# Splitting converted weights on GpSimd, and one attention product moved ahead, in a chunked-attention and gated-MLP kernel

## The chip, the cores and the metric

The kernel runs on one core of a Trainium2 chip. The core has five engines that work side by side, each with its own queue in order: TensorE (PE, matrix products), VectorE (DVE), ScalarE (ACT), GpSimd (POOL) and SyncE (SP, which here only issues DMAs). They work on SBUF, an on-chip memory of 128 partitions, and on PSUM, the banks into which PE writes. The metric is the time of one execution in microseconds (us) of device time.

## The reference

There are two parts. The first is attention within chunks of 64 positions, for 8 batches and 8 heads of 576 positions and 64 dimensions:

```
scores = scale * np.matmul(q_c, k_c.transpose(0, 1, 2, 4, 3))
attn = np.exp(scores - max); attn = attn / (sum + 1e-9)
out = np.matmul(attn, v_c)
```

Its result is read as x, 4608 tokens of 512 features. The second part is a gated MLP with 1536 hidden features:

```
gate = 1.0 / (1.0 + np.exp(-(x @ w_gate)))
val = x @ w_val
return (gate * val @ w_out).astype(np.float32)
```

All is float32. The weights are handed to the kernel as float64 bit patterns, two 32-bit words for each number.

## The kernel before

**Precision.** PE multiplies a 32-bit format with a shorter mantissa (float32r). So each factor of an MLP product is held as two parts, hi and lo: hi is the number cast to float32r, lo is what the cast left out. Each product is then three: hi with hi, hi with lo, lo with hi.

**Conversion of weights.** The weights are cut into 12 tiles f of 128 hidden features, and each tile has three parts of 128 x 512 numbers: gate (part 0), value (1) and out (2). `load_weights` (L99) brings a part's two words a number into a raw buffer by SP (L108). `convert_weights` (L110) makes hi and lo of it, in seven instructions: two multiplications by powers of two on ACT (L129, L130), a shift (L131), an and/or (L132) and an add (L134) on DVE, which together give the float32 number `val`; then the cast to hi on ACT (L136) and the subtraction val - hi = lo on DVE (L137). There are 36 conversions. For tiles 0 to 8 `val` lies in buffers of the weight pool that later tiles will use; from tile 9 on it lies in the pool `mp` under the tag "ob", which has two buffers. The raw buffers alternate too, so that the load of one tile's words waits for the conversion of an earlier one.

**Attention.** The work is cut into 36 units j = (block m of 512 tokens, half h of the block, group u of 4 heads). For a unit, `scores` (L177) multiplies q and k on PE (`products`, L170), takes the maximum on DVE, and either subtracts it there (op "S") or does subtraction, exponential and sum on ACT (op "s"); `softmax` ("E", L198) finishes the probabilities; `transposes` ("T" or "t", L211) turns them on PE and copies them back; `values` ("A", L224) multiplies by v (L231), and casts and subtracts the result into the hi and lo parts of x (L249 on ACT, L250 on DVE). Scores, transposes and products of values share two PSUM buffers (`ps_a`) in turn.

**MLP.** `hidden` ("H", L267) makes one tile f of hidden features for a block, or for one half ("a", "b") of it: 12 products with the gate weights (L261), a sigmoid on ACT (L270), 12 products with the value weights, the product of the two on DVE (hf, L272), and its hi (L274, ACT) and lo (hl, L276, DVE). `down` ("D", L281) multiplies these by the out weights into four accumulators (L287). Hidden features of tile f need all parts 0 and 1 of that tile, the down products need part 2.

**Order.** The strings START and MIDDLE list the first block's operations by hand: L and V are loads of q, k and v, W loads of weights ("u" for parts 0 and 1, "o" for part 2), C conversions ("C3.1" is part 1 of tile 3). In START, a planner that knows a cost for each instruction may still reorder each engine's queue, with the order of the string as priority. In MIDDLE the order of PE is as written and the other engines are planned; after it (`rest`, L642) PE and DVE are both as written.

**After the first block.** Blocks 1 and 2 go tile by tile in the same manner. Meanwhile POOL makes sums of the hi and lo weights (`keep_sums`, L331: L338, L344, a cast L346 and a subtraction L347), SP writes the weights and sums to DRAM (L324, L329), and blocks 3 to 8 are then done two at a time by a scheme with seven products in place of eight (L421, L496).

Of the kernel before, what the change touches and what calls it, by code (L numbers as in the profile page):

```python
# [8 lines left out]
F32 = mybir.dt.float32  # L9
# [3 lines left out]
ALU = mybir.AluOpType  # L13
# [13 lines left out]


START = """
L0 L1 V0 W0o S0 s1 V1 E0 W0u t0 C0.0 E1 L2 t1 L3 C0.1 A0 W1u S2 C0.2 s3 A1 C1.0 H0.0a E2 W1o E3 C1.1  # L30
T2 W2u T3 D V3 L4 V2 C2.0 A2 C1.2 A3 L5 H0.1a H0.0b W3o D W3u C2.1 C3.0 H0.1b D s4 W4u W2o H0.2 C3.2
C2.2 W4o C3.1 C4.0 D W5u E4 C4.1 C5.0 C5.1 H0.3 D s5 C4.2 t4 E5 W6u H0.4 D W7u C6.0 V5 W6o C7.0 C6.1
H0.5 D W5o L6 C5.2 L7 C6.2 H0.6 V4 W8u C7.1 D W7o C8.0 t5 C8.1 C7.2 H0.7 D W9u
# [15 lines left out]
def chunk_attn_moe(ctx: ExitStack, tc: tile.TileContext, q, k, v, w, out):  # L49


    nc = tc.nc
# [43 lines left out]
    def stage(tag, n):  # L96
        return wp.tile([P, n], U32, tag=tag, name="w_raw")
# [12 lines left out]
    def convert_weights(f, part):  # L110

        words = raws.pop((f, part)).rearrange("p (n two) -> p two n", two=2)
        low, high = words[:, 0, :], words[:, 1, :]
        if part == 0:
            both = wp.tile([P, 2, 1024], F32R, tag=f"u{f}", name="w")
            wt[f, 0], wt[f, 1] = both[:, :, :512], both[:, :, 512:]
        elif part == 2:
            wt[f, 2] = wp.tile([P, 2, 512], F32R, tag=f"o{f}", name="w")
        hi, lo = wt[f, part][:, 0], wt[f, part][:, 1]
        if f < 9:  # L120
            slot = 9 if f == 8 else 9 - f % 2
            if part == 0:
                spare[f] = stage(f"u{slot}", 2048)
            val = stage(f"o{slot}", 1024)[:, :512] if part == 2 else spare[f][:, 512 * part:512 * (part + 1)]
        else:
            val = mp.tile([P, 512], U32, tag="ob", name="w_val")


        nc.scalar.mul(val.bitcast(F32), high.bitcast(F32), 2.0 ** -112)  # L129
        nc.scalar.mul(low, low, 2.0 ** -29)  # L130
        nc.vector.tensor_scalar(out=val, in0=val, scalar1=3, scalar2=None, op0=ALU.logical_shift_left)  # L131
        nc.vector.scalar_tensor_tensor(  # L132
            out=val, in0=high, scalar=0x80000000, in1=val, op0=ALU.bitwise_and, op1=ALU.bitwise_or)
        nc.vector.tensor_tensor(out=val, in0=val, in1=low, op=ALU.add)  # L134
        val = val.bitcast(F32)
        nc.scalar.copy(hi, val)  # L136
        nc.vector.tensor_tensor(out=lo, in0=val, in1=hi.bitcast(F32), op=ALU.subtract)  # L137


    units = [(m, h, u) for m in range(NB) for h in range(2) for u in range(2)]  # L140
# [464 lines left out]
    def run(op):  # L605
        what, arg = op[0], op[1:]
        if what == "L":
            load(int(arg))
        elif what == "V":
            load_values(int(arg))  # L610
        elif what in "Ss":
            scores(int(arg), what == "s")
        elif what == "E":
            softmax(int(arg))
        elif what in "Tt":
            transposes(int(arg), what == "t")
        elif what == "A":
            values(int(arg))
        elif what == "W":
            load_weights(int(arg[:-1]), arg[-1])  # L620
        elif what == "C":
            f, part = arg.split(".")
            convert_weights(int(f), int(part))
        elif what == "H":
            m, f = arg.split(".")
            step(int(m), int(f.rstrip("ab")), f.lstrip("0123456789"))
        else:
            finish()
# [115 lines left out]
```

## Time and profile before

| what | value |
|---|---|
| median of 3 runs | 948.76 us (946.94 to 950.25) |
| the profiled execution | 949.0 us, of which span 947.2 us |
| PE busy | 927.4 us (98%) |
| DVE busy | 601.1 us (63%) |
| ACT busy | 340.5 us (36%) |
| POOL busy | 139.0 us (15%) |
| granted PE clock, mean | 0.994 |

The span runs from the first instruction to the last; the profiled execution's own time has 1.8 us around it. In the rows of the profile, "L137" is a line of the kernel, "lo<-val,hi" would name the tile written and those read, and "x18" a count of instructions. In the time line an instruction's start and duration stand first, and the idle time of its engine ahead of it, with what ended it, in square brackets. Buffer names: `w` is a weight's hi and lo pair, `w_raw` the raw words (and, for tiles 0 to 8, `val`), `w_val` is `val` of tiles 9 to 11.

### The profile page before, as it was taken

How to read it: one execution, taken by the hardware profiler on the slowest of the kernel's cores; microseconds unless marked ns; L12 is line 12 of the kernel's file. 1: busy time of each engine (PE TensorE's matmuls, PEld its weight loads, DVE VectorE, ACT ScalarE, POOL GpSimd, SP SyncE). 2: the span in 40 equal slices, each digit the busy share in tenths (PEclk: the TensorE clock that was granted, in tenths of full speed). 3: DMA queues.
4: the chain of work that ended last, by engine and by line, in shares of the span. 5: the costliest groups of instructions: out<-in, count | busy, mean ns of one | idle time of the engine just before them, and what ended most of it. 6: DMA issues, size and time to landing. Idle time of an engine off the chain costs nothing.

```text
span 947.2 us, 13080 instructions
## 1 busy us (share of the span) xinstructions
PE 927.4 (98%) x4960; PEld 762.0 (80%) x4960; DVE 601.1 (63%) x999; ACT 340.5 (36%) x556; POOL 139.0 (15%) x204
## 2 busy tenths in 40 slices
PE   6999999999999999999999999999999999999998
PEld 4778888888888887888887888888878888888886
DVE  6899973576576656766766666767686334445332
ACT  6899752233233242233142522232324221121222
POOL 1000006970079880000000000000000000000000
PEclk7999999999999999999999999999999999999999
DMA  8699894442243448657675756665565565556561
GB/s 290 210 305 298 313 305 168 134 145 78 64 137 112 134 141 312 203 200 229 205 246 207 254 186 219 211 220 201 190 222 197 193 208 183 203 184 215 218 222 45
DMA packets 81279, 189.61 MB, mean 200 GB/s; under 512 B 7488, under 2 KB 38208, under 8 KB 76608
## 3 DMA queue, kind: packets, MB, share of 16 engines
q1 hardware_dynamic: 81216, 188.77, 59.5%
q8 instruction: 39, 0.64, 0.3%
q14 instruction: 24, 0.20, 0.1%
HBM read 150.99 MB, written 37.75 MB: 199 GB/s over the span
## 4 chain that ended last, share of the span: by engine, by line
PE 81%; POOL 6%; DMA 6%; ACT 3%; DVE 2%; issue 1%; SPq 1%; POOLq 0%; ACTq 0%; DVEq 0%
PE acc L496 20%; PE cy L421 16%; PE g L261 13%; PE cz L421 11%; PE cx L421 10%; PE acc L287 6%; DMA sums<-a_both 3%; PE sc L170 3%; PE av L231 3%; POOL a_both L347 2%; POOL a_sum L344 2%; POOL a_both L346 1%; POOL a_val L338 1%; DMA out<-ob 1%; DMA wr<-sums 1%
## 5 line engine op out<-in xcount | busy, mean ns | idle before, releaser
L261 PE MATMUL g<-xt,w 128*128 128x512 f32 (+1 forms) x960 | 207.5, 371 | 3.0 <-ACT xt L249 1.3
L261 PEld LDWEIGHTS g<-xt,w 128*128 128x128 f32 x960 | 168.5, 189 | 36.3 <-ACT xt L249 1.7
L496 PE MATMUL acc<-wr,hh 128*128 128x512 f32 x576 | 177.8, 390 | 0.0
L421 PE MATMUL cy<-xc,wr 128*128 128x512 f32 x648 | 159.2, 389 | 0.9 <-DVE u L439 0.9
L421 PEld LDWEIGHTS cy<-xc,wr 128*128 128x128 f32 x648 | 121.5, 188 | 26.5 <-DVE u L439 1.3
L496 PEld LDWEIGHTS acc<-wr,hh 128*128 128x128 f32 x576 | 107.9, 188 | 22.7 <-ACT raw L242 0.3
L496 PE MATMUL acc<-wr,hl 128*128 128x512 f32 x288 | 112.7, 391 | 2.7 <-DVE hl L488 2.7
L421 PE MATMUL cz<-xc,wr 128*128 128x512 f32 x432 | 106.1, 391 | 1.1 <-DMA wr<-sums 1.1
L421 PE MATMUL cx<-xc,wr 128*128 128x512 f32 x432 | 106.0, 391 | 0.0
L560 DVE STREAM_TRANSPOSE pbd<-pr 32x256 f32<-32x256 f32 x224 | 97.6, 436 | 4.0
L488 DVE TENSOR_TENSOR hl<-hid,hh 128x512 fp32r<-128x512 f32 x72 | 49.5, 688 | 78.8 <-ACT hh L486 78.5
L421 PEld LDWEIGHTS cz<-xc,wr 128*128 128x128 f32 x432 | 80.5, 188 | 19.0 <-issue 2.5
L421 PEld LDWEIGHTS cx<-xc,wr 128*128 128x128 f32 x432 | 80.6, 188 | 17.5 <-issue 1.0
L287 PE MATMUL acc<-w,hh 128*128 128x512 f32 x288 | 90.4, 395 | 1.0 <-ACT hh L274 1.0
L486 ACT CAST hh<-hid 128x512 fp32r<-128x512 f32 x72 | 44.8, 622 | 127.1 <-PE acc L496 103.7
L338 POOL TENSOR_TENSOR a_val<-w 128x256 f32<-128x256 f32 x48 | 37.3, 798 | 202.2 <-ACT xt L249 144.7
L496 PEld LDWEIGHTS acc<-wr,hl 128*128 128x128 f32 x288 | 54.0, 188 | 16.0 <-DVE hl L488 4.8
L439 DVE TENSOR_TENSOR u<-cy,s 128x512 f32<-128x512 f32 x36 | 24.8, 688 | 63.3 <-PE cy L421 61.3
L272 DVE TENSOR_TENSOR hf<-g,hf 128x512 f32<-128x512 f32 (+1 forms) x40 | 25.4, 635 | 60.6 <-PE g L261 59.6
L287 PEld LDWEIGHTS acc<-w,hh 128*128 128x128 f32 x288 | 52.7, 188 | 13.1 <-issue 1.9
L456 DVE TENSOR_TENSOR u<-cy,s 128x512 f32<-128x512 f32 x36 | 24.9, 691 | 50.7 <-PE cy L421 50.5
L287 PE MATMUL acc<-w,hl 128*128 128x512 f32 x144 | 56.1, 389 | 0.0
(103 smaller groups left out, 1009.4 us busy)
## 6 DMA issues: line engine op xcount, KB each, us to landing
wr<-sums SPq DMA_DIRECT2D x72, 512.0 KB, 4.6
wr<-outer SPq DMA_DIRECT2D x36, 1024.0 KB, 4.9
w_raw<-w_in SPq DMA_DIRECT2D x36, 512.0 KB, 5.0
wr<-given SPq DMA_DIRECT2D x36, 512.0 KB, 3.7
sums<-a_both SPq DMA_DIRECT2D x24, 512.0 KB, 3.5
qt<-q_in SPq DMA_DIRECT2D x36, 256.0 KB, 4.4
kbd<-k_in SPq DMA_DIRECT2D x72, 128.0 KB, 4.4
vt<-v_in SPq DMA_DIRECT2D x36, 256.0 KB, 4.0
```

What stands on the lines that cost most here:

```text
L170: nc.tensor.matmul(sc[c * D:(c + 1) * D, (2 * a + t) * P:(2 * a + t + 1) * P], lhsT=s["qt"][:, a, n0:n0 + D], rhs=s["kb"][:, a, :, n0:n0 + D],
L231: nc.tensor.matmul(av[a * D:(a + 1) * D, c * P:(c + 1) * P], lhsT=s["vt"][:, a, c, :], rhs=pb[:, 4 * a + c, :, :], start=True, stop=True,)
L261: nc.tensor.matmul(ps[:, tok], lhsT=wt[f, which][:, wpart, c:c + P], rhs=x[:, part, i, tok], start=n == 0, stop=n == 11)
L272: nc.vector.tensor_tensor(out=hf, in0=pv, in1=hf, op=ALU.mult)
L287: nc.tensor.matmul(acc[m, t], lhsT=hx[:, ts], rhs=wt[f, 2][:, wpart], start=f == 0 and i == 0, stop=f == NF - 1 and i == 2,)
L338: nc.gpsimd.tensor_tensor(out=val[:, 2 * n:2 * n + 2], in0=parts[:, 0], in1=parts[:, 1], op=ALU.add)
L421: nc.tensor.matmul(bank, lhsT=lhs(wpart, c), rhs=x[:, part, c], start=start and k == 0, stop=stop and k == 5, skip_group_check=True)
L456: nc.vector.tensor_tensor(out=u3, in0=y, in1=s1, op=ALU.add)
L486: nc.scalar.copy(hh, h)
L488: nc.vector.tensor_tensor(out=hl, in0=h, in1=hh.bitcast(F32), op=ALU.subtract)
L496: nc.tensor.matmul(acc[m, t], lhsT=hx[:, ts], rhs=wo[f][:, wpart], start=f == 0 and i == 0, stop=f == NF - 1 and i == 2)
L560: nc.vector.transpose(out=pb[dst, :, c, h, i, :], in_=ps[src, h::2, k, :])
```

## The change

Two things are changed. First, in `convert_weights`, the cast to hi and the subtraction for lo go from ACT and DVE to POOL, for all conversions but the first (tile 0, part 0). Second, in the string START, the operation A1 (the product of unit 1's probabilities with v) stands right behind A0, ahead of W1u, S2, C0.2 and s3, where before it stood behind them.

```diff
-L0 L1 V0 W0o S0 s1 V1 E0 W0u t0 C0.0 E1 L2 t1 L3 C0.1 A0 W1u S2 C0.2 s3 A1 C1.0 H0.0a E2 W1o E3 C1.1
+L0 L1 V0 W0o S0 s1 V1 E0 W0u t0 C0.0 E1 L2 t1 L3 C0.1 A0 A1 W1u S2 C0.2 s3 C1.0 H0.0a E2 W1o E3 C1.1
...
         val = val.bitcast(F32)
-        nc.scalar.copy(hi, val)
-        nc.vector.tensor_tensor(out=lo, in0=val, in1=hi.bitcast(F32), op=ALU.subtract)
+        if (f, part) == (0, 0):
+            nc.scalar.copy(hi, val)
+            nc.vector.tensor_tensor(out=lo, in0=val, in1=hi.bitcast(F32), op=ALU.subtract)
+        else:
+            nc.gpsimd.tensor_copy(hi, val)
+            nc.gpsimd.tensor_tensor(out=lo, in0=val, in1=hi.bitcast(F32), op=ALU.subtract)
```

## The prediction

> **What bounds the kernel now.** The time slices of the page show TensorE (PE) full from the third slice of 23.7 us on: time can only be won or lost where it would stop. So I asked next for the table by stage, over the stretch where the weights are converted. Its columns are start and end, length, busy time of PE, weight loads, VectorE (DVE), ScalarE (ACT) and GpSimd (POOL), granted clock, DMA share and GB/s:
>
> ```profile
> 8.00:56.00 48.00, 39.78 (x300) 33.21 (x296) 41.36 (x86) 40.14 (x106) 0.00 (x0) 0.89 0.80 262
> 56.00:124.80 68.80, 68.80 (x330) 56.42 (x330) 64.84 (x119) 57.67 (x112) 0.00 (x0) 1.00 0.92 311
> ```
>
> From 8 to 56 us PE idles 48.00 - 39.78 = 8.2 us and is led by DVE and ACT, both over 80% busy. From 56 us on PE never stops, yet DVE is 64.84 / 68.8 = 94% busy, and POOL does nothing. Whether DVE has anything in hand shows where the last up tile (f = 11) takes its weights, in the timelines of DVE and PE:
>
> ```profile
> 123.41 1.46 DVE L137 TENSOR_TENSOR w<-w_val,w 128x512 fp32r<-128x512 f32 x2
> 124.81 5.60 PE L261 MATMUL g<-xt,w 128*128 128x512 f32 x24
> ```
>
> The gate and value weights of tile 11 are finished at about 124.1 and at 124.87. PE takes the gate half at 124.81 and the value half 2.8 us later: 0.7 and 2.7 us in hand. The conversions thus run at PE's pace, and whatever slows them by more than that stops PE.
>
> **The move to GpSimd.** Thirty-five of 36 conversions give their cast (L136) and subtraction (L137) to POOL. The groups of 56 to 124.8 us, counts behind "x", mean ns behind the comma:
>
> ```profile
> L137 DVE TENSOR_TENSOR w<-w_raw,w 128x512 fp32r<-128x512 f32 x18 | 12.2, 686 | 1.7 <-ACT w L136 1.7
> L134 DVE CUSTOM_DVE_ANT_0 w_raw<-w_raw 128x1024 uint16<-128x1024 uint16 x15 | 10.2, 683 | 0.0
> L132 DVE SCALAR_TENSOR_TENSOR w_raw<-w_raw 128x512 uint32<-128x512 uint32 x15 | 10.1, 685 | 0.0
> L131 DVE TENSOR_SCALAR w_raw<-w_raw 128x512 uint32<-128x512 uint32 x15 | 6.0, 420 | 0.0
> L132 DVE SCALAR_TENSOR_TENSOR w_val<-w_raw,w_val 128x512 uint32<-128x512 uint32 x8 | 5.5, 688 | 0.1
> L137 DVE TENSOR_TENSOR w<-w_val,w 128x512 fp32r<-128x512 f32 x8 | 5.5, 687 | 0.3 <-ACT w L136 0.2
> L134 DVE CUSTOM_DVE_ANT_0 w_val<-w_raw,w_val 128x1024 uint16<-128x1024 uint16 x8 | 5.5, 686 | 0.1
> L276 DVE TENSOR_TENSOR hl<-hf,hh 128x512 fp32r<-128x512 f32 x8 | 5.4, 680 | 0.1
> L131 DVE TENSOR_SCALAR w_val<-w_val 128x512 uint32<-128x512 uint32 x8 | 3.3, 424 | 1.4 <-ACT w_val L129 1.3
> ```
>
> Here 18 + 8 = 26 subtractions leave DVE, 12.2 + 5.5 = 17.7 us; the casts leave ACT. POOL's price for the same shapes and types is in its own later work (minimum/median/maximum ns):
>
> ```profile
> L346 POOL CAST a_both<-a_sum x24: 606/611/1614, 152.8 to 349.4; 128x512 fp32r<-128x512 f32 x24
> L347 POOL TENSOR_TENSOR a_both<-a_sum,a_both x24: 1275/1291/2150, 154.1 to 350.9; 128x512 fp32r<-128x512 f32 x24
> ```
>
> Alone, POOL needs 0.61 + 1.29 = 1.90 us a conversion, 26 x 1.90 = 49.4 us of the 68.8: it would fit. The maxima say what goes wrong. Rows of POOL and DVE that overlap:
>
> ```profile
> 269.61 0.73 POOL L338 TENSOR_TENSOR a_val<-w 128x256 f32<-128x256 f32 x1
> 270.30 1.29 POOL L347 TENSOR_TENSOR a_both<-a_sum,a_both 128x512 fp32r<-128x512 f32 x1
> 271.55 1.19 POOL L338 TENSOR_TENSOR a_val<-w 128x256 f32<-128x256 f32 x1
> ...
> 277.31 1.30 POOL L347 TENSOR_TENSOR a_both<-a_sum,a_both 128x512 fp32r<-128x512 f32 x1
> ```
>
> ```profile
> 203.28 0.88 POOL L344 TENSOR_TENSOR a_sum<-a_val 128x128 f32<-128x128 f32 x2
> ...
> 203.71 0.48 DVE L543 TENSOR_SCALAR sums<-sums 128x16 f32<-128x16 f32 x1
> ...
> 270.36 1.78 DVE L276 TENSOR_TENSOR hl<-hf,hh 128x512 fp32r<-128x512 f32 x1 [0.69 <-ACT hh L274]
> ...
> 277.58 0.68 DVE L272 TENSOR_TENSOR hf<-g,hf 128x512 f32<-128x512 f32 x1
> ...
> 288.17 0.17 DVE L543 TENSOR_SCALAR sums<-sums 128x16 f32<-128x16 f32 x1
> ```
>
> L276 reads two tiles of SBUF. Begun at 270.36 under a POOL subtraction it takes 1.78 us in place of 0.68 and ends at 272.14, 0.55 us after POOL's end at 271.59. POOL's next takes 1.19 in place of 0.73: it ends 0.60 us after DVE's end. The two exclude each other, whole instruction by whole instruction, with some 0.13 us (0.68 - 0.55, 0.73 - 0.60) saved at each handover. L272, which reads one operand in PSUM, is not touched (0.68 under 277.31). L543, a TENSOR_SCALAR with one input, is: 0.48 under the POOL pair of 203.28 to 204.16, against 0.17 at 288.17 with POOL not reading.
>
> Of a conversion, L132 and L134 read two SBUF tiles as L276 does and L131 is a TENSOR_SCALAR. No row shows these three beside a working POOL; by the nearest rows I take all of them as blocked. Their occupancy when back to back is the spacing of starts:
>
> ```profile
> 59.85 0.42 DVE L131 TENSOR_SCALAR w_raw<-w_raw 128x512 uint32<-128x512 uint32 x1
> 60.19 0.68 DVE L134 CUSTOM_DVE_ANT_0 w_raw<-w_raw 128x1024 uint16<-128x1024 uint16 x1
> 60.79 0.68 DVE L132 SCALAR_TENSOR_TENSOR w_raw<-w_raw 128x512 uint32<-128x512 uint32 x1
> ```
>
> That is 0.34 us for L131 and 0.60 for a 0.68 us operation. POOL's share, from handover to end, is 0.61 - 0.13 = 0.48 for the cast and 1.29 - 0.13 = 1.16 for the subtraction, 1.64 together. The port from 56 to 124.8 us then has to carry 23 x (0.34 + 0.60 + 0.60) = 35.4, plus 8 x 0.60 = 4.8 for L276, plus 26 x 1.64 = 42.6: 82.8 us in 68.8, so 14.0 us more even if it never rests. From above: DVE is in order, and if each POOL instruction stops it, it needs 64.84 - 17.7 + 42.6 = 89.7 us, 20.9 more. From below: if L131 goes free (its row has only 16 columns), 82.8 - 7.8 = 75.0, 6.2 more. I take 17, about the middle of the upper two, because POOL can run free only under the few one-input operations, and lose 1 of it to the 0.7 to 2.7 us in hand: +16.
>
> [...]
>
> What queues behind a blocked L131, L132 or L134 on DVE is the hf product (L272) and hl (L276), which PE's down products wait for; SyncE's next weight load, which waits for L134's release of the raw buffer, goes out later too. On POOL nothing is queued: its own sums come after this stretch (its first cast above is at 152.8).
>
> **Before 56 us.** Nine subtractions ran from 8 to 56 us, of which one stays, and ten casts, of which one stays.
>
> ```profile
> L137 DVE TENSOR_TENSOR w<-w_raw,w 128x512 fp32r<-128x512 f32 x9 | 6.2, 688 | 1.9 <-ACT w L136 1.8
> L131 DVE TENSOR_SCALAR w_raw<-w_raw 128x512 uint32<-128x512 uint32 x12 | 4.8, 421 | 0.7 <-ACT w_raw L129 0.5
> ...
> L136 ACT CAST w<-w_raw 128x512 fp32r<-128x512 f32 x10 | 6.2, 616 | 0.1
> ```
>
> ACT is relieved of 9 x 0.616 = 5.5 us and DVE of 8 x 0.688 = 5.5. Against that stand POOL's 8 x 1.64 = 13.1 us. Of DVE's remaining 35.9 us, 12 conversions at 1.54 (18.5 us) are of the blocked kind, half, so about half of POOL's time should stop it: 35.9 + 6.6 = 42.5 for 41.4 before. Bounds: 5.5 us won (ACT alone sets the pace) to 35.9 + 13.1 - 41.4 = 7.6 lost (every POOL instruction stops DVE). I take nothing won or lost, by the middle estimate.
>
> **Products of unit 1 ahead.** The move passes eight matrix products, a cast (L249) and a subtraction (L250) in front of the scores of units 2 and 3; it issues no DMA and passes no queue of SyncE or POOL. Rows of DVE, PE and ACT:
>
> ```profile
> 19.29 0.69 DVE L250 TENSOR_TENSOR xt<-av,xt 128x512 fp32r<-128x512 f32 x1
> 24.12 1.09 PE L231 MATMUL av<-pbd,vt 128*64 128x128 f32 x16
> 25.26 0.58 ACT L249 CAST xt<-av 128x512 fp32r<-128x512 f32 x1 [2.24 <-PE av L231]
> ```
>
> ACT idles 2.24 us until unit 1's product, begun at 24.12, is there. Done earlier, that idle time goes: 2.2 won. Against it, the scores of unit 2 then need the PSUM buffer (two in turn) that unit 0's L250 frees at 19.98, and those of unit 3 the one that unit 1's own L249 and L250 free; their softmax, and with it the second half of the tokens, shifts by the product, cast and subtraction put ahead, 1.09 + 0.58 + 0.69 = 2.4, to lose. Between -2.2 and +2.4 I take -1, nearer to the measured idle time, since a shift of the scores has DVE's and ACT's conversions to fill it.
>
> **Sum.** The profiled execution took 949.0 us (span 947.2 and 1.8 around it), 0.24 above the median of 948.76. 949.0 + 16 + 0 - 1 = 964.
>
> **Rivals.** (1) The free case, which ends on the other side: L131, L132 and L134 do not block. Then POOL's 49.4 us fit beside L276 alone, DVE loses 17.7 us of work, PE has no new wait after 56 us, and the start wins its full 5.5 and the 1 of unit 1, less 1.90 - 0.62 - 0.69 = 0.6 for the longer way through POOL: 949 - 5.9 = 943. It decides if L132 and L134 keep their 0.69 beside a busy POOL. For it: no row shows these forms blocked, and POOL is empty. Against: the pair at 270.30, whose DVE operation reads two SBUF tiles as these do. (2) The buffer chain: from tile 9 on, w_val has two buffers, each held to the end of the subtraction. From L131 on that is 0.42 + 0.69 + 0.69 + 0.61 + 1.29 = 3.70, and ACT's pass ahead of it (L129) some 0.62, by the cast of that size: 4.32. With each of the three DVE operations behind a POOL subtraction, 3 x 1.16 more: 7.8 us, 3.9 a conversion where the port allows 1.54 + 1.64 = 3.18. Over the eight w_val conversions that is 6 us on top of the upper bound: 949 + 20.9 + 6 - 1 = 975. It decides from 2 x 3.18 - 4.32 = 2.0 us of waits per conversion on. Against: before, its counterpart shows little (DVE waits 1.4 us in all for L129). (3) A draw: the port costs only the lower 6.2, less 1, and the start wins half of its bound, 2.7, and the 1 of unit 1: 949 + 5.2 - 3.7 = 950.5. DVE's idle time before L137 and L131 (1.7 and 1.4) speaks for it, its 94% against.
>
> **Chances.** Port-bound 62% (its own range 953 to 975), buffer chain 13%, a draw 8%, free 17%. The likeliest gives the predicted 964. The range runs from 947, below which the free case is left out, to 978, behind which I put 2%. A measurement of this kernel tells some 0.3% (2.8 us) from no change: faster 17% (the free case), same 7% (most of the draw), slower 76%.
>
> **What would show it.** In the changed profile, between 20 and 145 us, L132, L134 and L276 should have means of 1 us and more, POOL's subtraction a mean above 1.29, and PE new idle time of 10 us and more before products that take weights, released by POOL's part of w; the pair of tile 11 should be finished near 141 in place of 124.87. If L132 and L134 stay at 0.69 beside a busy POOL, the port step is wrong. If they grow and PE still doesn't stop, it is wrong that the conversions have nothing in hand. The cast of unit 1's product on ACT well before 25.26 would confirm the second part; a later softmax of units 2 and 3 with an empty ACT beside it would turn its sign. A different order of ACT, DVE and PE, which a planner sets in this part, could upset any of these.

## The result, and the profile after

The changed kernel takes 973.36 us in the median of six runs (972.03 to 975.7), the kernel before 948.9 (946.94 to 950.32) on the same chip: a ratio of 1.0262, 95% interval 1.0242 to 1.0283, or 24.5 us more. The forecast was slower, 964 us, in a range of 947 to 978. The profiled execution of the changed kernel has a span of 971.5 us, 24.3 more than the 947.2 before. In its rows some lines have moved: L140 and L141 are the cast and the subtraction on POOL, L265 the gate and value products (before L261), L274 the sigmoid (L270), L276 hf (L272), L278 its hi (L274) and L280 hl (L276).

The table by stage of the changed kernel, with the columns of the prediction:

```profile
8.00:56.00 48.00, 38.99 (x286) 32.78 (x287) 43.94 (x72) 35.63 (x85) 21.25 (x20) 0.89 0.76 256
56.00:124.80 68.80, 53.19 (x248) 41.91 (x247) 65.85 (x82) 41.21 (x89) 46.69 (x40) 0.90 0.60 205
```

Before 56 us PE is busy for 0.8 us less than before (38.99 against 39.78). From 56 to 124.8 us it stands still for 68.80 - 53.19 = 15.6 us, where it never stopped before, and its clock falls to 0.90. DVE, which lost all but one of its subtractions, is as busy as ever (65.85 against 64.84 us). The groups of that stretch say why:

```profile
L141 POOL TENSOR_TENSOR w<-w_raw,w 128x512 fp32r<-128x512 f32 x16 | 24.0, 1502 | 1.3
L132 DVE SCALAR_TENSOR_TENSOR w_raw<-w_raw 128x512 uint32<-128x512 uint32 x16 | 16.3, 1028 | 0.1
L134 DVE CUSTOM_DVE_ANT_0 w_raw<-w_raw 128x1024 uint16<-128x1024 uint16 x16 | 14.7, 926 | 0.1
L140 POOL CAST w<-w_raw 128x512 fp32r<-128x512 f32 x16 | 13.3, 830 | 17.3 <-DVE w_raw L134 17.3
L131 DVE TENSOR_SCALAR w_raw<-w_raw 128x512 uint32<-128x512 uint32 x14 | 10.4, 753 | 0.0
L280 DVE TENSOR_TENSOR hl<-hf,hh 128x512 fp32r<-128x512 f32 x5 | 5.8, 1168 | 0.1
```

All three DVE operations of a conversion, and hl, wait for POOL: means of 1028, 926, 753 and 1168 ns against 685, 683, 420 and 680 before. A conversion loses 0.34 + 0.24 + 0.33 = 0.92 us on DVE (unrounded means), more than the 0.69 that its subtraction took. Attention's small operations of eight columns, which the prediction's list of blocked work leaves out, wait too: L196 and L210 have means of 708 and 699 ns here, against 165 and 169 for the same operations before. POOL waits too: 1502 and 830 ns for operations that take 1291 and 611 alone.

When the last up tile has its weights, and when PE takes them, in the timelines of POOL and PE:

```profile
136.85 1.29 POOL L141 TENSOR_TENSOR w<-w_val,w 128x512 fp32r<-128x512 f32 x1
```

```profile
150.81 5.60 PE L265 MATMUL g<-xt,w 128*128 128x512 f32 x24
```

The pair of tile 11 is finished at 138.14, 13.3 us later than the 124.87 before. But PE takes it at 150.81, 26.0 later than 124.81. So only half of that delay is the weights' own. The waits of PE between 56 and 160 us (what for: us, times, longest) name the rest:

```profile
PE g L265 <- ACT hf L274: 8.3, 2, 5.8
PE g L265 <- DVE hf L276: 5.9, 2, 4.7
PE g L265 <- POOL w L140: 4.0, 2, 2.6
```

Most of it is not waiting for weights. PE waits 8.3 us for sigmoids (ACT) and 5.9 us for hf (DVE), which read a bank of gate or value products and so free it for the next. How hf comes late, in the timelines of DVE and PE of the changed kernel, and the row of the same hf (f = 7) in the kernel before:

```profile
109.30 0.82 DVE L131 TENSOR_SCALAR w_val<-w_val 128x512 uint32<-128x512 uint32 x1
110.16 1.63 DVE L132 SCALAR_TENSOR_TENSOR w_val<-w_raw,w_val 128x512 uint32<-128x512 uint32 x1
111.72 0.68 DVE L276 TENSOR_TENSOR hf<-g,hf 128x512 f32<-128x512 f32 x1
...
126.03 0.68 DVE L276 TENSOR_TENSOR hf<-g,hf 128x512 f32<-128x512 f32 x1
```

```profile
112.54 5.46 PE L265 MATMUL g<-xt,w 128*128 128x512 f32 x12 [4.72 <-DVE hf L276]
...
126.86 3.00 PE L265 MATMUL g<-xt,w 128*128 128x512 f32 x12 [1.19 <-DVE hf L276]
```

```profile
100.12 0.68 DVE L272 TENSOR_TENSOR hf<-g,hf 128x512 f32<-128x512 f32 x1
```

PE stands for 4.72 us until hf is through at 112.40. DVE has no idle time ahead of that hf: it works off conversions that stand ahead of it in its queue. At f = 7 hf starts at 126.03, 25.9 us later than before. And the queue itself has changed. The planner has moved conversions ahead of hf, as counted on DVE's queue (the number of L132 ahead of hf of f = 2 to 9):

```
               f2  f3  f4  f5  f6  f7  f8  f9
before         12  16  18  21  24  27  30  33
changed        14  17  21  24  29  33  35  36
```

The other large wait, 5.76 us at f = 3, has the same root one engine further on. Rows of DVE, ACT and PE:

```profile
53.54 2.26 DVE L131 TENSOR_SCALAR w_raw<-w_raw 128x512 uint32<-128x512 uint32 x2
55.73 0.68 DVE L185 TENSOR_REDUCE mx<-sc 128x8 f32<-128x512 f32 x1
```

```profile
57.16 1.28 ACT L199 ACT_TABLE_LOAD   x1 [3.70 <-DVE mx L196]
...
62.25 0.60 ACT L274 ACTIVATE hf<-g 128x512 f32<-128x512 f32 x1
```

```profile
62.99 7.52 PE L265 MATMUL g<-xt,w 128*128 128x512 f32 x24 [5.76 <-ACT hf L274]
```

Two shifts that take 2.26 us in place of 0.76 (0.34 + 0.42) stand ahead of unit 4's maximum on DVE. ACT stands 3.70 us for that maximum, then does the exponentials, and the sigmoid that PE waits for stands behind these.

### The profile page after: what moved, and what is told of

The parts are those of the page before. It is cut to its first block, busy times and chain, and to the rows that moved or that the text cites. A ratio compares the mean times of both kernels' runs of the same rounds, so it can differ in the third digit from the quotient of the medians.

```text
span 971.5 us, 13140 instructions
## 1 busy us (share of the span) xinstructions
PE 933.8 (96%) x4960; PEld 765.1 (79%) x4960; DVE 619.5 (64%) x964; ACT 325.2 (33%) x523; POOL 215.2 (22%) x274
## 4 chain that ended last, share of the span: by engine, by line
PE 84%; DVE 10%; issue 2%; ACT 1%; DMA 1%; POOL 1%; SPq 0%; DVEq 0%; ACTq 0%; POOLq 0%
PE acc L500 19%; PE cy L425 15%; PE g L265 15%; PE cz L425 10%; PE cx L425 10%; PE acc L291 8%; PE sc L174 3%; PE av L235 3%; DVE w_raw L132 2%; DVE w_raw L134 2%; DVE w_raw L131 1%; POOL w L141 1%; DVE hl L280 1%; POOL w L140 1%; DMA w_raw<-w_in 0%
## 5 line engine op out<-in xcount | busy, mean ns | idle before, releaser
L265 PE MATMUL g<-xt,w 128*128 128x512 f32 (+1 forms) x960 | 212.7, 377 | 23.3 <-ACT hf L274 8.3
L265 PEld LDWEIGHTS g<-xt,w 128*128 128x128 f32 x960 | 170.8, 192 | 59.4 <-issue 15.3
L276 DVE TENSOR_TENSOR hf<-g,hf 128x512 f32<-128x512 f32 (+1 forms) x40 | 25.4, 634 | 67.2 <-PE g L265 66.2
```

Source lines behind the costliest of these rows:

```text
L265: nc.tensor.matmul(ps[:, tok], lhsT=wt[f, which][:, wpart, c:c + P], rhs=x[:, part, i, tok], start=n == 0, stop=n == 11)
L276: nc.vector.tensor_tensor(out=hf, in0=pv, in1=hf, op=ALU.mult)
```

## The experiments

The theory after this reading: the exclusion of DVE and POOL makes the weights some 14 us late, and the rest is the order of work on DVE, in which hf stands behind the slowed conversions. Rivals: a longer way through POOL without exclusion (latency), the two buffers of w_val, the products of unit 1. All ratios below are to the kernel before on the same chip.

**Does POOL's reading alone cost it?** Kernel before, with 24 pairs of cast and subtraction on POOL on a tile that nobody else uses, from the start of the program. Their sum goes nowhere, so no data wait for POOL, and DVE's queue is that of before (12, 16, 18, 21, 24, 27, 30, 33).

```diff
+    scratch = xp.tile([P, 4, 512], F32, tag="x", name="scratch")
+    nc.gpsimd.memset(scratch[:, 0], 0.0)
+    for _ in range(24):
+        nc.gpsimd.tensor_copy(scratch[:, 1], scratch[:, 0])
+        nc.gpsimd.tensor_tensor(out=scratch[:, 2], in0=scratch[:, 0], in1=scratch[:, 1], op=ALU.subtract)
```

> The kernel before with 24 casts and 24 subtractions of 128x512 on GpSimd that run from the start on and that nothing reads (own buffer, so no engine waits for them). Port theory: 24 x 1.64 = 39 us of port time fall on VectorE's conversions between about 5 and 85 us, L131, L132, L134 and L137 stretch to means of 0.8 us and more while GpSimd runs, and the time rises by 15 to 35 us, to 964 to 984. Latency theory (the split is slow because a weight's hi and lo now come 0.6 us later each, over two engines): nothing waits for this work, 949 within 1.5.

Measured: 968.19 us, ratio 1.0186 (1.0161 to 1.021). The groups of 8 to 124.8 us (here L137 is the and/or, L139 the add, L136 the shift) and POOL's own rows (minimum/median/maximum ns):

```profile
L137 DVE SCALAR_TENSOR_TENSOR w_raw<-w_raw 128x512 uint32<-128x512 uint32 x27 | 22.5, 844 | 0.2
L139 DVE CUSTOM_DVE_ANT_0 w_raw<-w_raw 128x1024 uint16<-128x1024 uint16 x27 | 21.9, 816 | 0.2
L136 DVE TENSOR_SCALAR w_raw<-w_raw 128x512 uint32<-128x512 uint32 x27 | 17.4, 664 | 0.0
```

```profile
L85 POOL COPY scratch<-scratch x24: 610/691/960, 5.1 to 60.7; 128x512 f32<-128x512 f32 x24
L86 POOL TENSOR_TENSOR scratch<-scratch x24: 1264/1585/1793, 5.8 to 61.5; 128x512 f32<-128x512 f32 x24
```

All three forms grow beside POOL work that they share no data with, to 844, 816 and 664 ns from 686, 684 and 420 in the same stretch of the kernel before: the exclusion holds for each, the shift too, and latency isn't needed to explain a loss of this size (that theory expected 949 within 1.5). Note the place: these pairs run from 5 to 63 us, in the start, where the prediction put POOL's cost at nothing, and cost 18 us there, with three times the eight pairs that the change has in it.

**And writing alone?** Kernel before with 80 memsets of 128 x 512 on POOL from the start.

```diff
+    scratch = xp.tile([P, 4, 512], F32, tag="x", name="scratch")
+    for _ in range(40):
+        nc.gpsimd.memset(scratch[:, 1], 0.0)
+        nc.gpsimd.memset(scratch[:, 2], 0.0)
```

> The kernel before with 80 fills of 128x512 on GpSimd in the same place, which write SBUF and read nothing; nothing reads them. If the exclusion is about reading: L132, L134 and L137, with two inputs, keep 0.69 us, L131 alone may stretch, and the time is 949 to 954. If any GpSimd work excludes VectorE: as the reading work, 960 and more.

Measured: 979.40 us, ratio 1.0306 (1.028 to 1.0332), from one instruction. A row of DVE, and the memsets:

```profile
9.56 32.44 DVE L196 TENSOR_SCALAR mx<-mx 128x8 f32<-128x8 f32 x1
```

```profile
L85 POOL MEMSET scratch<- x40: 529/532/535, 5.0 to 41.4; 128x512 f32 x40
```

A TENSOR_SCALAR of eight columns, 0.16 us in the kernel before (L192), stands for 32.44 us and ends at 42.00, when the last memset ends (41.4 + 0.53 = 41.9). Beside the reading POOL work of the changed kernel DVE got its turn after one instruction (no operation up to 160 us takes more than 1.78 us); against these memsets it got none. Whether that is due to the writing or to the missing gap isn't separated: a memset starts every 0.47 us, before the last one's 0.53 us are over, where the reading instructions leave 0.06 to 0.09 us between them. What two-input operations do beside writes isn't shown either: they stood in the queue behind this one. So neither expectation fits as it was meant: the time is that of the second, from a single wait that neither named.

**The split alone, and the products of unit 1 alone.** The diffs are the second and the first part of the change.

> The split on GpSimd alone; unit 1's product stays where it was before. Port theory (GpSimd and VectorE exclude each other on the conversion's operations): the whole slowdown is here, 972 to 976, as the changed kernel's 973.4 give or take what the moved product is worth (predicted 1 us won). Order theory (the moved product, and what the planner makes of it, upsets the start; the changed profile has PE 7 us late at tile 3 already): a good part of the 24.5 us goes, 955 to 967.

> The moved product alone; all conversions stay on ScalarE and VectorE. Prediction: 1 us won, between 2.2 won and 2.4 lost, so 946.5 to 951. Order theory: 955 or more, the start is upset by the move itself.

Measured: the split alone 977.33 us, ratio 1.0282 (1.0248 to 1.0317); the products ahead alone 954.38, ratio 1.0044 (1.0027 to 1.0061). Both lie just outside what was expected (972 to 976, and 946.5 to 951 or 955 and more). So the split carries the loss, and the products ahead, alone, cost 4 us too (0.0044 x 949, 2.6 to 5.8), where I had put -1. In the split alone PE's waits up to 200 us lie elsewhere: the longest, 8.5 us, is for probabilities that DVE finishes (L213), and those for hf come to 3.6 us. Together with the split their effect can't be told from nothing: 1.0262 against 1.0282, with overlapping intervals. Where they lose alone, in the rows of ACT and PE:

```profile
24.11 1.28 ACT L270 ACT_TABLE_LOAD   x1
...
25.81 1.28 ACT L195 ACT_TABLE_LOAD   x1
...
29.43 0.66 ACT L136 CAST w<-w_raw 128x512 fp32r<-128x512 f32 x1
```

```profile
30.14 0.58 PE L261 MATMUL g<-xt,w 128*128 128x256 f32 x1 [4.81 <-ACT w L136]
```

The first sigmoid now lies ahead of the exponentials of s3 on ACT, and the exponential of unit 2 (L201) behind them, at 30.25 in place of 21.81; at the sigmoid and again at the exponentials behind it ACT loads a table (1.28 us each, at 24.11 and 25.81), and a cast of weights, for which PE stands 4.81 us, lies behind them. The next kernel keeps the products ahead, and holds that sigmoid back behind the last exponential of s3:

```diff
+            last_exp[j] = nc.scalar.activation(
...
-        nc.scalar.activation(hf, pg, AF.Sigmoid)
+        with tc.issue_after(last_exp[3]) if (m, f) == (0, 0) else ExitStack():
+            nc.scalar.activation(hf, pg, AF.Sigmoid)
```

> Only the products with v of unit 1 ahead, nothing on POOL, and ScalarE is made to issue the sigmoid of the first hidden part (L270) behind the last exponential of s3, as in the kernel before. Theory A (the 5 us that the products ahead cost alone come from that sigmoid, which lands ahead of s3's exponentials, adds two table loads of 1.28 us and puts a cast of weights behind eight exponentials): 947 to 951. Theory B (the loss is in TensorE's order itself): 953 to 956, as without the edit.

Measured: 951.33 us, ratio 1.0032 (1.0014 to 1.005): 3.0 us, between the two theories. The wait of 4.81 us is gone, but another of 3.35 us, put down to DVE's work on the softmax, stands ahead of the place:

```profile
28.45 0.63 PE L216 MATMUL tp<-ident,early 128*128 128x128 f32 x4 [3.35 <-DVE sums L207]
29.57 1.10 PE L262 MATMUL g<-xt,w 128*128 128x256 f32 x3 [0.49 <-ACT w L136]
```

The interval overlaps that of the products alone, and a loss against the kernel before remains. That ACT's order decides where PE waits is seen in the rows; how large a part of the price it is isn't settled.

**Cast or subtraction?** Only the cast on POOL (with the products ahead, and without), and only the subtraction (with them).

```diff
-            nc.gpsimd.tensor_tensor(out=lo, in0=val, in1=hi.bitcast(F32), op=ALU.subtract)
+            nc.vector.tensor_tensor(out=lo, in0=val, in1=hi.bitcast(F32), op=ALU.subtract)
```

```diff
-            nc.gpsimd.tensor_copy(hi, val)
+            nc.scalar.copy(hi, val)
```

> As the changed kernel, but the subtraction for lo goes back to VectorE; only the cast for hi is on GpSimd. Port theory: VectorE keeps its 0.60 and gets 0.48 of waiting a conversion, 26 x 0.48 = 12.5 us from 56 to 124.8 us on 64.84 busy, 77.3 in 68.8: 8.5 us more, scaled by measured over predicted (24.5 for 16) up to 13: 956 to 962. Latency theory: the cast takes 0.61 there and 0.62 on ScalarE, so within 2 of 949.

> Only the cast of the high part on POOL (tiles after the first), the subtraction stays on VectorE, the products with v of unit 1 stay in their old place. Theory A (a one-input cast hardly holds VectorE up: the run with this and the products ahead took 954.0, no more than 954.4 for the products ahead alone): 947.5 to 951, no difference from before. Theory B (the cast's price was hidden there behind that of the products ahead; by the port it is 24 casts of 0.6 us in the stretch that counts): 953 to 958.

> As the changed kernel, but the cast for hi goes back to ScalarE; only the subtraction for lo is on GpSimd. Port theory: VectorE loses 0.60 and gets 1.16 of waiting a conversion: 64.84 - 17.7 + 26 x 1.16 = 77.3 in 68.8, the same 8.5 to 13 more as with the cast alone: 956 to 962. Latency theory: 0.6 us later for each lo, and lo is the last to be used: 949 to 952.

Measured: cast alone, products ahead, 954.04, ratio 1.0056 (1.0037 to 1.0075); cast alone, products in the old place, 953.60, ratio 1.0052 (1.0032 to 1.0072); subtraction alone, products ahead, 964.98, ratio 1.0163 (1.0132 to 1.0195). The first falls between its two theories, the third above the 956 to 962 of the port theory. The groups of 56 to 124.8 us for the second, and of 8 to 160 us for the third:

```profile
L140 POOL CAST w<-w_raw 128x512 fp32r<-128x512 f32 x17 | 15.4, 914 | 38.1 <-DVE w_raw L134 38.1
...
L132 DVE SCALAR_TENSOR_TENSOR w_raw<-w_raw 128x512 uint32<-128x512 uint32 x16 | 11.0, 699 | 0.0
L131 DVE TENSOR_SCALAR w_raw<-w_raw 128x512 uint32<-128x512 uint32 x15 | 7.4, 497 | 0.7 <-ACT w_raw L129 0.7
```

```profile
L141 POOL TENSOR_TENSOR w<-w_raw,w 128x512 fp32r<-128x512 f32 x26 | 41.9, 1621 | 60.2 <-ACT w L140 60.2
L134 DVE CUSTOM_DVE_ANT_0 w_raw<-w_raw 128x1024 uint16<-128x1024 uint16 x27 | 24.7, 920 | 0.4
L132 DVE SCALAR_TENSOR_TENSOR w_raw<-w_raw 128x512 uint32<-128x512 uint32 x27 | 22.5, 844 | 0.3
```

The subtraction is the dear half: it holds DVE up by 0.24 and 0.16 us in the two-input operations of a conversion, and the shift by 0.24 (664 ns against 420). With the cast the wait falls mostly on POOL (914 ns in place of 611); DVE's and/or keeps 699, its shift grows by 0.08 to 497 and its own subtraction to 771. Still the cast costs 5 us without the products ahead, in the range of theory B: I had read it as free from the first of these runs, because the products ahead cost as much alone. That these 5 us are the exclusion's is argued, not shown: in that run PE's waits from 56 to 124.8 us are for the sigmoid (3.0 us), and before 56 us it is busy for 1.9 us less than before.

**Which conversions?** Tiles 9 to 11 (those with the two w_val buffers) back on ACT and DVE; then only tiles 0 to 2 on POOL.

```diff
-        if (f, part) == (0, 0):
+        if (f, part) == (0, 0) or f >= 9:
```

```diff
-        if (f, part) == (0, 0):
+        if (f, part) == (0, 0) or f > 2:
```

> As the changed kernel, but tiles 9 to 11 are split on ScalarE and VectorE again; 26 conversions stay on GpSimd. Port theory: the nine give back their share, 9/35 of 24.5 or some 6 us: 965 to 969. Buffer theory (from tile 9 on GpSimd holds the two w_val buffers too long, and that sets the end): most of the loss goes, 950 to 958.

> As the changed kernel, but only tiles 0 (parts 1 and 2), 1 and 2 are split on GpSimd, 8 conversions. Prediction's step for the start: nothing won or lost within -5.5 and +7.6, middle +1.2, less 1 for the product: 946 to 952. If the 7 us that PE is late at tile 3 in the changed kernel come from the start and are not made up later: 954 to 957.

Measured: 969.63, ratio 1.0214 (1.0181 to 1.0246), and 952.27, ratio 1.0036 (1.0019 to 1.0052). The stretch of 56 to 124.8 us in each:

```profile
56.00:124.80 68.80, 53.96 (x253) 42.63 (x252) 67.61 (x90) 44.72 (x97) 37.70 (x33) 0.90 0.66 222
```

```profile
56.00:124.80 68.80, 66.67 (x321) 53.96 (x320) 62.37 (x116) 56.65 (x118) 0.00 (x0) 0.98 0.89 303
```

Without POOL on the last three tiles PE still idles 14.8 us (68.80 - 53.96), and the time is next to the 965 to 969 of the port theory and far from the 950 to 958 of the buffers: the two buffers aren't the main cause. The eight conversions of tiles 0 to 2 cost nothing that the runs can tell beyond the products ahead alone (1.0036 against 1.0044, with overlapping intervals).

**Is it the order on DVE?** Two kernels do the whole change, but say where conversions stand in DVE's queue. In the first each conversion is issued behind the hf that precedes it in the program's list (`gate` holds the hf instructions):

```diff
+    gate = []
...
-        nc.vector.tensor_scalar(out=val, in0=val, scalar1=3, scalar2=None, op0=ALU.logical_shift_left)
+        with tc.issue_after(gate[-1]) if gate else ExitStack():
+            nc.vector.tensor_scalar(out=val, in0=val, scalar1=3, scalar2=None, op0=ALU.logical_shift_left)
...
-        nc.vector.tensor_tensor(out=hf, in0=pv, in1=hf, op=ALU.mult)
+        gate.append(nc.vector.tensor_tensor(out=hf, in0=pv, in1=hf, op=ALU.mult).ins)
```

> The change whole, but VectorE is made to issue each product of the hidden part (hf, L276) ahead of the conversions that stand behind it in the program's list, so that about as many conversions lie ahead of each hf as in the kernel before (counted on VectorE's queue up to hf of f4: 18 before, 21 in the changed kernel, 17 here; f7: 27, 33, 26). Same work on every engine. Theory A (the port makes each conversion wait, which is 14 us by itself; the rest of the 24 us comes because VectorE works in order and hf, whose end frees the bank of the next value half, stands behind more and slower conversions): 958 to 967, TensorE's idle time behind hf gone between 56 and 140 us, and the waits of TensorE put down to POOL's part of w instead. Theory B (the order is of no account; the conversions are late wherever they stand): 970 to 976, as the changed kernel.

Measured: 983.62 us, ratio 1.0363 (1.0341 to 1.0384), a miss: worse than the change. The waits of PE (56 to 200 us) and of DVE (56 to 160 us); hf is L279, the value half L268, POOL's cast L143:

```profile
PE g L268 <- POOL w L143: 7.9, 4, 3.9
PE acc L294 <- POOL w L143: 6.2, 2, 3.6
```

```profile
DVE hf L279 <- PE g L268: 14.6, 2, 8.2
```

Now DVE stands 14.6 us at hf for a value half, PE in turn stands for weights, and the conversions that would make those weights wait in the queue behind that hf. This kernel overshot: it has 9 to 35 conversions ahead of hf of f = 2 to 11, where the kernel before has 12 to 36. The second sets exactly that kernel's numbers, 12, 16, 18, 21, 24, 27, 30, 33, 35, 36 from f = 2 to 11:

```diff
+    gate, made = [], [0]
+    quota = [4, 7, 9, 9, 12, 16, 18, 21, 24, 27, 30, 33, 35, 36]
...
-        nc.vector.tensor_scalar(out=val, in0=val, scalar1=3, scalar2=None, op0=ALU.logical_shift_left)
+        made[0] += 1
+        before = [hf for hf, n in zip(gate, quota) if n < made[0]]
+        with tc.issue_after(before[-1]) if before else ExitStack():
+            nc.vector.tensor_scalar(out=val, in0=val, scalar1=3, scalar2=None, op0=ALU.logical_shift_left)
...
-        nc.vector.tensor_tensor(out=hf, in0=pv, in1=hf, op=ALU.mult)
+        gate.append(nc.vector.tensor_tensor(out=hf, in0=pv, in1=hf, op=ALU.mult).ins)
```

> The change whole, with the number of conversions ahead of each hf on VectorE's queue set to the same as in the kernel before: 12, 16, 18, 21, 24, 27, 30, 33, 35, 36 ahead of hf of f2 to f11 (the changed kernel has 14, 17, 21, 24, 29, 33, 35, 36, 36, 36; the run in which hf stood as early as the program's list allows has 9, 14, 17, 20, 22, 26, 29, 32, 33, 35, and took 983.6). Theory A (the 10 us of the loss beyond my sum of 14 came from the six more conversions that lie ahead of hf of f7 in the changed kernel; 9 to 35 in the earlier run overshot, so that conversions stood behind an hf whose weights they were): 960 to 967, hf of f7 about 14 us later than before's 100.12 where the changed kernel has 25.9 later. Theory B (VectorE, slowed to one conversion in 3 us, is the bound either way: what hf gains, the weights lose, and the ring from VectorE over POOL and TensorE back to VectorE adds its waits): 970 to 984, with waits for POOL's part of w on TensorE and of VectorE for TensorE's value half that the changed kernel does not have.

Measured: 966.64 us, ratio 1.0179 (1.0144 to 1.0214). The time is that of theory A: with the conversions at their old places in DVE's queue the change costs 17 us (0.0179 x 949), and restoring them gives back 0.0262 - 0.0179 = 0.0083, some 8 us (2.7 to 13 by the ends of the two intervals). Rows of DVE (hf of f = 7 is L282), POOL and PE:

```profile
108.14 0.68 DVE L282 TENSOR_TENSOR hf<-g,hf 128x512 f32<-128x512 f32 x1
```

```profile
140.73 1.29 POOL L147 TENSOR_TENSOR w<-w_val,w 128x512 fp32r<-128x512 f32 x1
```

```profile
122.16 7.05 PE L271 MATMUL g<-xt,w 128*128 128x512 f32 x24 [4.89 <-ACT hf L280]
...
140.34 5.60 PE L271 MATMUL g<-xt,w 128*128 128x512 f32 x24
```

At f = 7 hf is 8.0 us late (108.14 against 100.12), not the 14 of theory A, where the changed kernel has 25.9. The pair of tile 11 is finished at 142.02, even later than in the changed kernel (138.14), yet PE takes it at 140.34, 15.5 late in place of 26.0. Between f = 7 and f = 11 the delay doubles. PE's waits from 56 to 160 us still aren't for weights; nearly all are for the sigmoid:

```profile
PE g L271 <- ACT hf L280: 7.3, 3, 4.9
```

And there ACT's rows show another wait:

```profile
111.59 0.69 ACT L132 ACTIVATE w_val<-w_raw 128x512 f32<-128x512 f32 x1 [5.92 <-POOL w L147]
...
120.31 0.67 ACT L132 ACTIVATE w_val<-w_raw 128x512 f32<-128x512 f32 x1 [4.90 <-POOL w L147]
...
121.45 0.56 ACT L280 ACTIVATE hf<-g 128x512 f32<-128x512 f32 x1
```

ACT (here L132 for L129) stands for a w_val buffer that POOL's subtraction holds, 4.90 us, with the sigmoid behind it, and PE's 4.89 us at 122.16 are for that sigmoid. From 105 to 130 us four such waits of ACT come to 17.0 us (5.92 + 4.90 + 1.65 + 4.57), against 4.3 from 56 to 160 us in the changed kernel and 1.0, for DVE's subtraction, in the kernel before. So the 17 us are not the exclusion alone: the buffer chain, the second rival, has a share in the last tiles. And as this wait grew when DVE's order was restored, the 8 us are what restoring it gave back on balance, not the full price of the order. A third buffer wasn't tried, and how the 17 us divide stays open.

None of the versions is faster than the kernel before.

## Why the prediction was right or wrong

**The exclusion: right in kind.** What the prediction calls the port is DVE and POOL excluding each other; no run shows a port itself. That L131, L132 and L134 are blocked was an estimate from the nearest rows (L276 with 1.78 us in place of 0.68, L543 with 0.48 in place of 0.17), and under which operations POOL runs free, on which the choice of 17 rests, no run shows. L132 and hl grew past 1 us, POOL's subtraction to 1.50, PE got 15.6 us of idle time. L134 stayed at 0.93, just under the 1 us that I named. Tile 11's pair was finished at 138.14, not "near 141": 13.3 us, where the sum had 16 after the slack; the bare sum of 14.0 came nearer than the middle of the upper two. A conversion lost 0.92 us on DVE, not the 1.64 of the bound from above, since POOL bears a part of the waits itself. That bound also takes off 0.68 us a subtraction where the prediction's own spacing of starts gives 0.60, so that it should be 2 us higher.

**The step that failed** is the sentence on what queues behind a blocked conversion. It names hf and hl and gives them no price; the sum goes on as if PE could only lose by late weights, and "what would show it" expects its idle time to be released by POOL's part of w. That was 4.0 us; 14.2 (8.3 + 5.9) were released by the sigmoid and hf. The order, which the last sentence names as something that "could upset" the rest, is the missing term: some 8 us by the run with the order restored, which came out at 966.6, close to the forecast of 964. The closeness is partly luck, since the buffer chain, priced apart from it, has a part in those 17 us. It is luck in part, too, that the 24.5 us of the change stayed in the range: they are more than the 20.9 of the bound from above, and fitted only through the room left for other terms.

**A term not in the sum: PE's clock.** After the waits of 5.76 and 4.72 us PE was slower: 12 products took 5.46 us at 112.54 against 3.00 at 126.86, 2.5 us, and the 24 of f = 3 took 7.52 us at 62.99 against 5.73 before, 1.8 us. The row of f = 3 in the kernel before, and windows of the changed kernel:

```profile
55.80 5.73 PE L261 MATMUL g<-xt,w 128*128 128x512 f32 x24 [0.37 <-ACT hf L270]
```

```profile
60.00:68.00 8.00, 5.01 (x14) 4.05 (x15) 7.76 (x11) 6.51 (x16) 5.56 (x6) 0.57 0.87 307
...
112.00:116.00 4.00, 3.46 (x8) 2.81 (x9) 3.67 (x5) 1.90 (x3) 3.84 (x4) 0.50 1.07 401
```

The windows have granted clocks of 0.57 and 0.50. After the wait of 1.19 us the 12 products took 3.00 us; how long a wait must be to slow PE isn't shown.

**The start** at nothing: held, as far as the runs can tell, for what the change puts there, by the run with tiles 0 to 2 alone (1.0036 against 1.0044). Not because POOL is harmless there: 24 pairs in the start cost 18 us.

**The products of unit 1** at -1, bounds -2.2 to +2.4: wrong alone, 4 us lost (2.6 to 5.8), outside the bounds. Unit 1's cast did come early (in the changed kernel it ends at 19.92, where the kernel before begins it at 25.26). With the products alone the softmax of unit 2 came later, as I had named, but not beside an empty ACT: the sigmoid and the exponentials of unit 3 stand ahead of it in ACT's queue, and I hadn't priced such a change of places. Within the change it is worth nothing that the runs can tell.

**The rivals.** The free case fell with the 24 idle pairs on POOL and with the means of L131, L132 and L134. The buffer chain was not what decides, by the run without POOL on tiles 9 to 11 (1.0214, PE idle 14.8 us), but it shows on ACT in the changed kernel (4.3 us) and grew to 17.0 us once the order was restored. The draw fell with the 17 us.

## What to carry to other kernels

Expect work that leaves a busy VectorE for GpSimd to come back as waits: here, where both read SBUF, 0.69 us of subtraction a conversion went and 0.92 us of waits came. Price also what stands behind each slowed instruction in its in-order queue, and look at how a planner will set that queue anew: restoring the old order gave back 8 us, and putting the blocked work last cost 10 more. Which of two reading instructions bears the wait differs: the two-input subtraction of 1.3 us mostly stopped VectorE (0.64 us a conversion against 0.33 on itself), the cast of 0.6 us mostly itself (0.30 against some 0.18). Whether the length or the number of inputs decides was not separated.

## What was not expected of the hardware

A VectorE TENSOR_SCALAR of 128 x 8, 0.16 us long, stood for 32.44 us beside GpSimd memsets of 0.53 us each that followed one another without a gap, while beside GpSimd work that reads, waits ended with one instruction (the longest single VectorE operation up to 160 us in the changed kernel took 1.78 us). The exclusion of L131, a shift with one input, was taken from a row of 16 columns, and holds in full size: 753 ns against 420.
